# Block-sparse attention in front of a gated FFN: sampled key and value blocks gathered on GpSimd in place of dense masked scores

## The chip, the cores and the metric

The kernel runs on one core of a Trainium2 chip. The metric is device time in microseconds (us) of one execution; lower is better. The kernel before takes 371.69 us (median of three runs, 371.41 to 374.39). Engines are named as the profile names them: PE (TensorE matmuls), PEld (TensorE weight loads, which overlap PE), DVE (VectorE), ACT (ScalarE), POOL (GpSimd), SP (SyncE, which here only issues DMAs).

## The reference

The reference is a block-sparse attention over 4 batches, 8 heads, 768 tokens and head size 64, followed by a gated feed-forward network (FFN) over all 3072 tokens.

```python
block, n_blocks, window = 32, 24, 1
scores = scale * q @ k.T                                   # per batch and head, 768 x 768
mask = abs(blk_i - blk_j) <= window                        # local blocks
mask |= (blk_i == 0) | (blk_j == 0) | (blk_i == 23) | (blk_j == 23)   # global blocks
for qb in range(24):
    for kb in sampled_blocks[qb]:                          # 3 sampled key blocks a query block
        mask[qb*32:(qb+1)*32, kb*32:(kb+1)*32] = True      # same for all heads and batches
attn = softmax(where(mask, scores, -1e9))
x = (attn @ v) laid out as (3072, 512)
out = (sigmoid(x @ w_gate) * (x @ w_val)) @ w_out          # 512 -> 1536 -> 512, float32
```

Each of the 22 inner query blocks needs at most 8 of the 24 key blocks: three local, two global, three sampled. The sampled ones are known only at run time, from a tensor of 24 x 3 integers.

## The kernel before: the parts that matter

It computes all scores, takes the exponential of all of them, and multiplies by a mask of zeros and ones. Two heads share one score tile of 128 keys (twice) by 512 columns.

```python
def scores(n, p, tt):                 # n: 256 queries of a batch, p: head pair, tt: 256 keys
    st = ps.tile([128, 2, 512], f32, tag="st", bufs=2, name="st")
    for jj in range(2):
        for hd in range(2):
            nc.tensor.matmul(st[:, hd, jj*CH:(jj+1)*CH], kT[r, j, :], qT[r, 2*c:2*c+2, :], ...)
def exps(n, p, tt):                   # 144 of them
    nc.scalar.activation(pt, sts.pop((n, p, tt)), AF.Exp, scale=SCALE)
def masks(n, p, tt):                  # 144 of them
    nc.vector.tensor_tensor(pt, pt, m.unsqueeze(1).to_broadcast([128, 2, 512]), op=ALU.mult)
def values(n, p):
    # 12 matmuls of V against pt, 256 columns each (the output is already x transposed),
    # then 24 matmuls of a column of ones against pt, 128 columns each: the row sums
    # [cut]
def recips(n, p):                     # 48 of them, 128 x 128
    nc.vector.reciprocal(rz, pvz[n, p][:, CH : CH + 128])
# spread(): two matmuls copy the reciprocals to all partitions; norm(): x = xu * rb   [cut]
```

The schedule gives each slot two pieces of attention and about as much FFN work, so from the first quarter of the run on PE always has FFN matmuls to do while ACT and DVE work at the softmax:

```python
while items or s < NS:
    credit = min(credit, 0.0) + (FFN_FIRST if s < 20 else FFN_SLOT)
    # [cut: take FFN items while there is credit, interleave them with scores, exps, masks, values]
```

The softmax here doesn't subtract the row's maximum and nothing guards it: scores larger than these inputs give would overflow.

## Time and profile before

| | before |
|---|---|
| median of three runs | 371.69 us |
| span of the profiled execution | 366.4 us |
| PE, DVE, ACT, POOL busy | 318.9, 236.4, 202.3, 45.0 us |
| first FFN activation result (`h`) on DVE | 42.8 us after the start |

The page of the kernel before: each engine's busy time with its share of the span and its instructions, and three rows of the picture in 40 slices of 9.2 us (a digit is the busy tenths of a slice; PEclk is the granted TensorE clock in tenths).

```profile
PE 318.9 (87%) x3476; PEld 173.5 (47%) x3476; DVE 236.4 (65%) x395; ACT 202.3 (55%) x281; POOL 45.0 (12%) x61
...
PE   3766777758999969999999999999999998999994
...
POOL 8720022220000222200002222000000000000000
PEclk9986999999999999999999999999999999999999
```

PE is at nine tenths or more in most slices from the eleventh on and is the limit there. The chain of work that ended last, on the same page, says the same:

```profile
PE 65%; DVE 4%; ACT 3%; issue 2%; DVEq 0%
```

The costliest groups of ACT and DVE before (line, engine, operation, output and input, count; then busy us and mean ns of one; then idle time just before them and what ended it):

```profile
L228 ACT ACTIVATE pt<-st 128x1024 f16<-128x1024 f32 x144 | 146.3, 1026 | 69.8 <-PE st L217 69.6
L234 DVE TENSOR_TENSOR pt<-pt,mask 128x1024 f16<-128x1024 f16 x144 | 102.4, 711 | 63.2 <-ACT pt L228 63.2
...
L276 DVE RECIPROCAL rz<-pvz 128x128 f16<-128x128 f32 x48 | 45.9, 957 | 16.1 <-ACT xu L281 13.7
```

The exponentials and masks are large, but both groups stood idle waiting for PE: they hide behind it. A stretch of PE's timeline in the middle (start, duration, instruction) shows what PE does:

```profile
203.08 0.38 PE L355 MATMUL py<-wo,h_2356 128*128 128x512 f16 x1
203.39 0.61 PE L217 MATMUL st<-qT,kT 64*128 64x256 f16 x8
203.93 0.85 PE L247 MATMUL pvz<-pt,v_2080 128*64 128x256 f16 x12
204.70 0.52 PE L260 MATMUL pvz<-pt,ones 128*32 128x128 f16 x24
205.16 0.39 PE L323 MATMUL gv<-x_2282,wg 128*128 128x512 f16 x1
```

Matmuls are pipelined, so start-to-start times are the cost: 8 score matmuls 0.54 us, 12 value matmuls 0.77 us, 24 row-sum matmuls 0.46 us, and there is no gap. To make this kernel faster, PE must get less work, or start its full work sooner.

### The profile page before, as it was taken

To read this page: it belongs to the slowest core of one execution; us is meant where nothing else is said; L and a number is where in the kernel's file an instruction comes from. 1 tells how busy PE (TensorE), PEld (TensorE's weight loads), DVE (VectorE), ACT (ScalarE), POOL (GpSimd) and SP (SyncE) were. 2 spreads that over 40 slices of the span, in tenths; PEclk is the share of its full clock that TensorE was granted. 3 is DMA by queue.
4 is the path that set the end of the run, shared out by engine and by line. 5 is a ranking of instruction groups with operands and counts; after the bars stand their busy time and mean duration, and the time that the engine had idled before them with its cause. 6 is when DMAs were issued, how large, how long until landed. Compare 5 with 4: busy or idle time off the path is not lost.

```text
span 366.4 us, 8250 instructions
## 1 busy us (share of the span) xinstructions
PE 318.9 (87%) x3476; PEld 173.5 (47%) x3476; DVE 236.4 (65%) x395; ACT 202.3 (55%) x281; POOL 45.0 (12%) x61
## 2 busy tenths in 40 slices
PE   3766777758999969999999999999999998999994
PEld 2433545533454535445445544545554454446641
DVE  4576677777586667768657786866867677434321
ACT  1845665676666775665656666566667555221110
POOL 8720022220000222200002222000000000000000
PEclk9986999999999999999999999999999999999999
DMA  8999667760003778500004697300010000001011
GB/s 116 200 207 207 115 142 163 159 115 2 0 2 113 155 150 171 79 31 30 2 30 109 171 181 166 73 1 30 2 59 2 30 2 30 29 31 57 33 64 77
DMA packets 40897, 30.56 MB, mean 83 GB/s; under 512 B 20740, under 2 KB 37788, under 8 KB 40860
## 3 DMA queue, kind: packets, MB, share of 16 engines
q1 hardware_dynamic: 29580, 20.59, 20.5%
q0 software_dynamic: 11280, 9.44, 18.0%
q8 instruction: 27, 0.44, 0.5%
q14 instruction: 10, 0.08, 0.1%
HBM read 28.45 MB, written 6.29 MB: 95 GB/s over the span
## 4 chain that ended last, share of the span: by engine, by line
PE 65%; DVE 4%; ACT 3%; issue 2%; DVEq 0%
PE gv L323 31%; PE py L355 16%; PE pvz L247 7%; PE st L217 6%; PE pvz L260 4%; ACT pt L228 2%; DVE y L364 2%; ACT tg L334 1%; PE pvz L288 1%; DVE rz L276 1%; DVE pt L234 1%; DVE x_2282 L307 0%; ACT xu L281 0%; DVE x_2284 L307 0%; DVE h_3493 L339 0%
## 5 line engine op out<-in xcount | busy, mean ns | idle before, releaser
L228 ACT ACTIVATE pt<-st 128x1024 f16<-128x1024 f32 x144 | 146.3, 1026 | 69.8 <-PE st L217 69.6
L234 DVE TENSOR_TENSOR pt<-pt,mask 128x1024 f16<-128x1024 f16 x144 | 102.4, 711 | 63.2 <-ACT pt L228 63.2
L334 ACT ACTIVATE tg<-gv 128x512 f32<-128x512 f32 (+1 forms) x84 | 45.3, 539 | 37.9 <-PE gv L323 35.8
L276 DVE RECIPROCAL rz<-pvz 128x128 f16<-128x128 f32 x48 | 45.9, 957 | 16.1 <-ACT xu L281 13.7
L217 PE MATMUL st<-qT,kT 64*128 64x256 f16 x576 | 48.4, 278 | 6.0 <-ACT pt L228 3.7
L323 PEld LDWEIGHTS <-wv 128*128 128x128 f16 x336 | 32.8, 98 | 36.1 <-issue 6.9
L323 PEld LDWEIGHTS <-wg 128*128 128x128 f16 x336 | 28.2, 97 | 31.3 <-issue 8.0
L281 ACT COPY xu<-pvz 128x256 f32<-128x256 f32 x48 | 17.9, 373 | 33.3 <-PE pvz L260 32.5
L217 PEld LDWEIGHTS <-kT 64*128 64x128 f16 x576 | 21.9, 95 | 24.4 <-issue 15.4
L260 PE MATMUL pvz<-pt,ones 128*32 128x128 f16 x1152 | 25.5, 224 | 0.0
L364 DVE TENSOR_SCALAR y<-py 128x512 f32<-128x512 f32 x24 | 16.6, 690 | 12.1 <-PE py L355 11.1
L288 PE MATMUL pvz<-rz,sel 128*128 128x128 f16 x96 | 13.2, 218 | 12.1 <-DVE rz L276 12.1
L260 PEld LDWEIGHTS <-ones 128*32 128x32 f16 x1152 | 17.0, 98 | 9.9 <-issue 9.9
L288 PEld LDWEIGHTS <-sel 128*128 128x128 f16 x96 | 9.4, 97 | 22.7 <-issue 14.7
L137 ACT COPY qT<-ptr 128x768 f16<-128x768 f16 x4 | 3.2, 797 | 8.8 <-PE ptr L130 8.8
L196 PE MATMUL pm<-mb_127,e_70 24*128 24x256 f16 x18 | 4.3, 364 | 3.9 <-DVE mask L203 2.8
L203 DVE CAST mask<-pm 128x512 f16<-128x512 f32 x9 | 5.9, 685 | 0.8 <-PE pm L196 0.7
L105 POOL CAST q_3157<-qs 128x768 f16<-128x768 f32 x1 | 0.8, 823 | 44.9 <-DMA qs<-in_q_dram 44.9
L105 POOL CAST q_1956<-qs 128x768 f16<-128x768 f32 x1 | 0.8, 823 | 41.6 <-DVE pt L234 41.6
L323 PE MATMUL gv<-x_326,wg 128*128 128x256 f16 x12 | 3.3, 278 | 2.3 <-ACT tg L334 2.3
L323 PE MATMUL gv<-x_1478,wv 128*128 128x512 f16 x12 | 4.5, 379 | 0.7 <-ACT tg L334 0.7
L323 PE MATMUL gv<-x_3071,wv 128*128 128x512 f16 x12 | 4.5, 379 | 0.7 <-ACT tg L334 0.7
(435 smaller groups left out, 567.1 us busy)
## 6 DMA issues: line engine op xcount, KB each, us to landing
out_dram<-y SPq DMA_DIRECT2D x24, 256.0 KB, 2.0
qs<-in_q_dram SPq DMA_DIRECT2D x12, 384.0 KB, 4.6
ks<-in_k_dram SPq DMA_DIRECT2D x12, 384.0 KB, 5.0
wg<-in_moe_w_gate_dram POOLq DMA_DIRECT2D x3, 512.0 KB, 12.2
wv<-in_moe_w_val_dram POOLq DMA_DIRECT2D x3, 512.0 KB, 13.8
wo<-in_moe_w_out_dram POOLq DMA_DIRECT2D x3, 512.0 KB, 19.9
kf<-in_k_dram POOLq DMA_DIRECT2D x4, 192.0 KB, 6.7
qf<-in_q_dram POOLq DMA_DIRECT2D x4, 192.0 KB, 6.9
```

The source lines that it names most:

```text
L217: nc.tensor.matmul(st[:, hd, jj * CH : (jj + 1) * CH], kT[r, j, :], qT[r, 2 * c : 2 * c + 2, :], start=True, stop=True,)
L228: nc.scalar.activation(pt, sts.pop((n, p, tt)), AF.Exp, scale=SCALE)
L234: nc.vector.tensor_tensor(pt, pt, m.unsqueeze(1).to_broadcast([128, 2, 512]), op=ALU.mult)
L247: nc.tensor.matmul(t[hd * 64 : hd * 64 + 64, 0:CH], v_[:, hd, j, :], pts[j // 2][:, hd, (j % 2) * CH : (j % 2 + 1) * CH], start=(j == 0), ...
L260: nc.tensor.matmul(t[r0 : r0 + 32, CH : CH + 128], ones, pts[j // 2][:, hd, o : o + 128], start=False, stop=(j == NJ - 1), skip_group_chec ...
L276: nc.vector.reciprocal(rz, pvz[n, p][:, CH : CH + 128])
L281: nc.scalar.copy(xu, pvz[n, p][:, 0:CH])
L288: nc.tensor.matmul(rb[:, half * 128 : half * 128 + 128], sel[:, half, :], rz, start=True, stop=True, skip_group_check=True,)
L323: nc.tensor.matmul(t[:, 0 : cols(g)], w[:, i, f * 128 : (f + 1) * 128], xT[g, i][:, 0 : cols(g)], start=(i == 0), stop=(i == NP - 1),)
L334: nc.scalar.activation(t[:, 0 : cols(g)], pgs.pop((g, f)), AF.Tanh, scale=0.5)
L355: nc.tensor.matmul(pys[g, tt], hts[g, f][:, tt * 128 : (tt + 1) * 128], wo[:, f], start=(f == 0), stop=(f == NF - 1),)
L364: nc.vector.tensor_scalar_mul(y, pys.pop((g, tt)), 0.5)
```

## The change

The intent is to compute only the scores that the reference keeps. Per head pair (a "unit"; 16 of them, 4 a batch) the scores fall from 9 tiles of 128x1024 to 5. Local and global keys are two tiles of 128 keys for every four query blocks; the sampled blocks, three a query block, are gathered. A column of ones beside V makes the row sums a 65th column of the value matmuls. So the ones-matmuls, the big reciprocals, the spreading matmuls and most of the mask work go.

The price is on GpSimd. Each unit gathers 90 key blocks of 16 words along the free dimension (66 sampled, and 24 fixed ones, which the two-tile layout needs a second time), and for each of its two heads 30 value blocks of 32 words (22 columns of sampled blocks, 6 of fixed ones, 2 of padding). The value blocks must first be copied to all four groups of 32 partitions, by 32 SBUF-to-SBUF DMAs a batch.

```diff
+    def spread_v(b, half):                       # twice a batch, 16 DMAs each
+        for a in range(4):
+            for s in range(4):
+                nc.sync.dma_start(v4[half][32 * s : 32 * s + 32, a:NB:4]..., va[b % 2][32 * a : 32 * a + 32, ...]...)
+    def gather_k(u):                              # 2 x 45 blocks of 16 words
+        for i in range(2):
+            nc.gpsimd.indirect_copy(t...[:, 45 * i : 45 * i + 45], data, idx[:, i, 0:3], i_know_this_is_slow=True)
+    def gather_v(u):                              # 2 x 30 blocks of 32 words
+        for hd in range(2):
+            nc.gpsimd.indirect_copy(vg[u % 2][hd]...[:, :, 0 : D // 2], data[...], idx[:, 2, 0:2], i_know_this_is_slow=True)
+    def scores(u, x):                             # five pieces a unit
+        if x < 3:                                 # local keys, then the tile of fixed keys, from kg
+            ...
+                mm(i, 0, kT[u][:, t * 128 : t * 128 + 128], qs, n)
+                c = (3 * NQ + 4 * t) * BLK
+                mm(i, n, kg[u][:, c : c + 128], qs, n)
+        else:                                     # sampled keys, 64 columns a matmul
+            for r in range(16) if x == 3 else range(16, NQ):
+                mm(r // 8 % 2, r % 8 * 64, kg[u][:, c : c + 128], z[:, r + 1], 64)
+        nc.scalar.activation(pt[:, 0:w], st..., AF.Exp, scale=SCALE)
+        # [cut: masks for x < 3]
+    def values(u, half):                          # 65 columns a matmul: V and a one
+        # [cut]
+        nc.vector.reciprocal(rz, pvv[:, :, :, 64])
+    def pieces(b):                                # one batch's attention, in order
+        def prep(u):
+            return [lambda: (turn(u, "k"), gather_k(u)), lambda: (turn(u, "q"), gather_v(u))]
+        r += prep(first)
+        for u in us:
+            w = u - 1                                        # the unit before
+            a = [lambda u=u, x=x: scores(u, x) for x in (0, 1, 3, 2, 4)]
+            z = [] if u == first else ends(w)                # values, x_turn, values, x_turn of w
+            n = prep(u + 1) if u < last else []
+            for s in (a[0], z[0], a[1], n[0], z[1], a[2], z[2], a[3], n[1], a[4], z[3]):
+                if s: r.append(s)
-    # [cut: the slot-by-slot schedule with credit]
+    for s in pieces(0): s()                       # all of batch 0's attention before any FFN
+    for b in range(B):                            # batch b's FFN with batch b+1's attention mixed in
+        lo, hi = (0.5, 0.97) if b == 0 else (0.05, 0.95)
+        # [cut: pieces(b+1) spread between the fractions lo and hi of the FFN; spread_v(b+1) just before them]
+        # [cut: at the end of the block, the loads of batch b+2, issued by GpSimd]
```

`turn` transposes q or k of a unit on PE; `x_turn` transposes the attention output into the FFN's layout. FFN tiles become 384 columns wide instead of 512.

## The prediction

> **What bounds the kernel now.** The page gives PE 318.9 us busy of a 366.4 us span (87%), DVE 236.4, ACT 202.3, POOL 45.0, and the chain that ended last is 65% PE. In the slices PE is at 9 tenths or more from about 80 us on; the timeline there shows 128x512 matmuls 0.216 us apart with almost no gap. Before that PE is starved: 4.0, 6.9, 6.5, 6.8 us busy in the first four stretches of 10 us, the clock at 0.7 to 0.8 from 20 to 40 us.
>
> **What changes.** Scores fall from 144 exps of 128x1024 (1.026 us) to 80, masks from 144 (0.711 us) to 32 full and 32 part ones, the 48 reciprocals of 0.957 us become 32 tiny ones, the xu copies vanish. Added: turns of q and k on PE with copies on DVE and ACT, 32 turns of x. My sums: ACT about 145 us, DVE about 165 us. Neither was the limit, so that is worth little.
>
> PE: the FFN is the same arithmetic (384-column tiles instead of 512), about 187 us at the pitch seen. Attention now costs, per 12 score matmuls 0.66, values 0.7, sums 0.45, spread 0.21 us: about 2.0 us x 48 = 97 us. After: 640 score matmuls, half of them 64 or 128 columns wide, 1280 of 65 columns, 512 small transposes; at 25 to 55 ns each about 5.2 us x 16 = 83 us. PE work falls by only 10 to 20 us.
>
> **What is new on the critical path: GpSimd.** Each of 16 head pairs needs four gathers: 90 key blocks of 16 words, 60 value blocks of 32 words, 3360 words per partition. The trace's POOL cast (128x768, 0.82 us) gives 1.07 ns a word: 3.6 us. The Trainium skill (GPSIMD Engine Reference, Performance pitfalls for Q7 kernels) puts a small read command, one per gather index, at about 102 cycles that do not pipeline: 150 of them would be 12.8 us at 1.2 GHz; no run here shows it yet. If a command takes several indices it is a third of that. Estimate: 10 us a pair (8 to 16), 160 us in all.
>
> The whole attention of batch 0 now precedes any FFN. The first value gather waits for 6 fine-grained v loads and 16 SBUF-to-SBUF copies, about 33 us; seven more gather steps of 5 us and the last values bring the FFN's start to about 76 us, PE mostly idle and cold. Batch 1's attention is packed into the second half of the first FFN: about 10 us of stall. Later batches have about 67 us of PE work each against about 60 us of POOL work and loads: 3 to 8 us of stall each. Sum: 76 + (38 + 21 + 10) + 2 x (67 + 5) + 54 + 3, about 346, less a little for rounding up: I say 344. Each us more per pair costs about 12 us in total.
>
> **What the profile would show.** POOL busy 150 to 200 us; indirect copies of 2 to 3 us each; DVE and ACT under 50%; PE under 3 tenths until about 75 us, then above 9 tenths with dips where PE waits for kg or vg; the FFN's first matmul near 76 us.
>
> **What would make it wrong.** A gather of 4 us or more (16 us a pair): POOL then bounds every batch and the kernel is slower, near 410. Gathers of 1.5 us: near 310. Small matmuls with exposed weight loads at 80 ns rather than 40 would add 40 us.
>
> Chances: faster 0.67, within 2% 0.10, slower 0.23. Predicted 344 us, range 306 to 398.

## The result, and the profile after

The prediction was wrong in its direction: the kernel became slower.

| | before | after |
|---|---|---|
| median (four runs each) | 371.55 us | 417.37 us |
| lowest to highest | 369.38 to 374.39 | 417.13 to 418.48 |
| ratio, after over before | | 1.123 (95%: 1.116 to 1.131) |
| span of the profiled execution | 366.4 us | 416.7 us |

Some executions of a program run slower, at a lower granted clock; only fast ones are compared. A ratio here and below is the mean time of one kernel's fast runs over the mean of the other's of the same rounds, so it is not quite the ratio of the medians quoted beside it. Every experiment was timed beside the kernel before on its own chip; before's median was between 370.2 and 372.5 us in every group of runs.

The page of the kernel after (slices of 10.4 us), the same rows:

```profile
PE 313.5 (75%) x3584; PEld 193.5 (46%) x3584; DVE 176.8 (42%) x349; ACT 137.3 (33%) x193; POOL 146.4 (35%) x133
...
PE   1140656899744876969189999959699999999984
...
POOL 8415533680043544850443359024433410000000
PEclk9999756589968999998869999979699999999999
```

The chain that ended last, after:

```profile
PE 53%; issue 12%; POOL 11%; DMA 9%; DVE 8%; ACT 3%; SPq 2%; DVEq 0%; POOLq 0%
```

PE did not fill up at 80 us and stay full. It has holes in every batch, down to one tenth in the slice around 205 us. POOL is recorded as busy for only 35% of the span, yet POOL, "issue" and DMA now hold 32% of the chain where before "issue" alone had 2%. The groups that answer to those shown of before, and the new ones of GpSimd:

```profile
L331 ACT ACTIVATE pt<-st 128x1024 f16<-128x1024 f32 (+1 forms) x80 | 79.8, 1002 | 148.3 <-PE st L296 148.2
...
L342 DVE TENSOR_TENSOR pt<-pt,mask 128x1024 f16<-128x1024 f16 (+1 forms) x64 | 39.4, 636 | 115.5 <-ACT pt L331 115.4
L277 POOL INDIRECT_COPY vg<-v,idx 128x960 uint32 x32 | 57.8, 1807 | 76.6 <-issue 48.1
...
L262 POOL INDIRECT_COPY kg<-kT,idx 128x720 uint32 x32 | 39.4, 1232 | 109.8 <-issue 51.4
```

The intended savings are all there: 67 us less of exponentials, 63 us less of masks, and the 45.9 us of reciprocals became 6.2. They were off the critical path and bought nothing directly. And the two gather groups have about 50 us each of idle time before them, called "issue", in which the engine waited for nothing that the profile shows. What PE waited for (what, for which releaser, us in total, times, longest):

```profile
PE st L296 <- POOL kg L262: 57.1, 12, 12.9
PE st L296 <- DVE qz L256: 9.6, 5, 5.4
```

Twelve waits for gathered keys make up 57.1 us; no other wait comes near.

### Where the 73 us between prediction and result lie

DVE's `h` instruction ends each FFN step, 24 of them a batch. So the start of the 1st, 25th, 49th and 73rd `h` cut the run into a head, three blocks (one batch's FFN with the next batch's attention mixed in) and a rest. These cuts are used for every experiment below. The predicted row is the prediction's sum: an FFN start at 76 us and about 3 us to the first `h`, and its terms for the blocks.

| us | head, to first `h` | block of batch 0 | block 1 | block 2 | rest |
|---|---|---|---|---|---|
| predicted | 79 | 69 | 72 | 72 | 54 |
| after | 88.4 | 90.0 | 90.5 | 85.5 | 62.2 |
| missed by | +9.4 | +21.0 | +18.5 | +13.5 | +8.2 |

(The predicted row adds up to 346, which I had rounded to 344; the after row adds up to the span of 416.7, within rounding.) Each of the three blocks, not just the head, is far longer than predicted. The rest is 8 us longer for reasons that no experiment moves: it is 62 to 63 us in all of them. In the trace the matmuls there are as fast as I had summed: the eight of an FFN step take 1.30 us, and four output matmuls 0.86 us. What my 54 + 3 left out are stalls: about 0.23 us at every fourth step, and 0.95 us before each of the last three outputs, where PE waits until DVE has read the one `py` buffer; together 4.2 us. The run also ends 5 us after the last matmul, not 3. Most of what is left of the 8 us is the cut: the first `h` comes only 1.5 us after the FFN's start there, not 3.

### How long is a gather?

GpSimd's timeline in the head of the kernel after (start, duration, instruction, idle time before it and what ended that):

```profile
14.66 1.20 POOL L262 INDIRECT_COPY kg<-kT,idx 128x720 uint32 x1 [2.31 <-issue]
17.95 1.20 POOL L262 INDIRECT_COPY kg<-kT,idx 128x720 uint32 x1 [2.08 <-issue]
27.95 1.60 POOL L277 INDIRECT_COPY vg<-v,idx 128x960 uint32 x1 [8.80 <-DMA v<-va]
31.31 1.60 POOL L277 INDIRECT_COPY vg<-v,idx 128x960 uint32 x1 [1.77 <-issue]
```

The same view later, where batch 2's attention is computed:

```profile
186.98 1.20 POOL L262 INDIRECT_COPY kg<-kT,idx 128x720 uint32 x1 [2.09 <-issue]
197.59 1.88 POOL L277 INDIRECT_COPY vg<-v,idx 128x960 uint32 x1 [9.41 <-PE gv L434]
201.24 1.60 POOL L277 INDIRECT_COPY vg<-v,idx 128x960 uint32 x1 [1.77 <-issue]
204.91 1.20 POOL L262 INDIRECT_COPY kg<-kT,idx 128x720 uint32 x1 [2.07 <-issue]
```

A key gather is recorded as 1.20 us, but two of them in a row start 3.29 us apart (14.66 and 17.95); two value gathers start 3.36 us apart. The Trainium skill (Perfetto Trace Analysis, GPSIMD Engine Instruction) says that a GpSimd span is unreliable and that consecutive instructions should be timed by the spacing of their starts; this trace agrees, and by a factor of more than two. A unit's four gathers so take 2 x 3.28 + 2 x 3.37 = 13.3 us, where I had predicted 10.

### What does PE wait for?

The second of these timelines is the heart of the case. PE, in the same place:

```profile
199.28 0.27 PE L296 MATMUL st<-qz,kT 128*128 128x256 f16 x1
209.45 0.40 PE L296 MATMUL st<-qz,kg 128*128 128x256 f16 x1 [9.90 <-POOL kg L262]
```

PE stood still for 9.9 us for the key gathers of batch 2's second unit. The keys to be gathered lay ready: DVE copied that kT at 193.54, for 0.95 us. But the key gathers had been issued behind the value gathers of the first unit, and those waited for the spread copies of V. SP issued these 32 copies one by one:

```profile
182.13 22.96 SPq L144 DMA_DIRECT2D v<-va  x32
```

The 16th, the last that the first unit needs, was issued at 193.17 us and landed at 195.46; the value gather's record begins 2.1 us later, of which 1.77 us is the gap that precedes any such gather here. (The timeline names "PE gv L434" as what ended that wait. It is an inference from semaphores, and the copies explain the time better.) The Trainium skill (TensorE: Matmul & The Clock Gate, Part 1) says that GpSimd's queue is strictly first in, first out, on each of its cores; the trace agrees, as the key gathers, ready at about 194.5 us, did not begin until the two value gathers were done, at about 202.8.

So there were two theories after the result. **Size**: the gathers are a third longer than predicted, and POOL is simply the limit. **Order**: GpSimd has time enough, but things are issued in an order in which one waiting gather holds up another and PE behind it. A third, **data**: the loads and the spread of V come late, and the gathers only show it.

### The profile page after: what moved, and what is told of

The parts are those of the page before. It is cut to its first block, busy times and chain, and to the rows that moved or that the text cites. A ratio compares the mean times of both kernels' runs of the same rounds, so it can differ in the third digit from the quotient of the medians.

```text
span 416.7 us, 8409 instructions
## 1 busy us (share of the span) xinstructions
PE 313.5 (75%) x3584; PEld 193.5 (46%) x3584; DVE 176.8 (42%) x349; ACT 137.3 (33%) x193; POOL 146.4 (35%) x133
## 3 DMA queue, kind: packets, MB, share of 16 engines
q1 hardware_dynamic: 30640, 19.53, 19.4%
## 4 chain that ended last, share of the span: by engine, by line
PE 53%; issue 12%; POOL 11%; DMA 9%; DVE 8%; ACT 3%; SPq 2%; DVEq 0%; POOLq 0%
PE gv L434 23%; PE py L454 14%; PE st L296 7%; DMA v<-va 7%; POOL kg L262 6%; PE pv L357 6%; POOL vg L277 3%; SPq L144 2%; ACT pt L331 2%; PE ptr L245 2%; DVE pt L342 2%; DVE kT L251 1%; DMA va<-in_v_dram 1%; POOL va L135 1%; DVE y L463 1%
## 5 line engine op out<-in xcount | busy, mean ns | idle before, releaser
L331 ACT ACTIVATE pt<-st 128x1024 f16<-128x1024 f32 (+1 forms) x80 | 79.8, 1002 | 148.3 <-PE st L296 148.2
L296 PE MATMUL st<-qz,kg 128*128 128x64 f16 (+1 forms) x448 | 45.5, 228 | 62.9 <-POOL kg L262 57.1
L342 DVE TENSOR_TENSOR pt<-pt,mask 128x1024 f16<-128x1024 f16 (+1 forms) x64 | 39.4, 636 | 115.5 <-ACT pt L331 115.4
L277 POOL INDIRECT_COPY vg<-v,idx 128x960 uint32 x32 | 57.8, 1807 | 76.6 <-issue 48.1
L445 DVE SCALAR_TENSOR_TENSOR h<-tg,gv 128x384 f16<-128x384 f32 x96 | 53.1, 553 | 74.0 <-PE gv L434 66.3
L434 PE MATMUL gv<-x,wg 128*128 128x384 f16 x384 | 82.4, 339 | 0.0
L434 PE MATMUL gv<-x,wv 128*128 128x384 f16 x384 | 80.7, 334 | 1.8 <-DVE h L445 1.0
L443 ACT ACTIVATE tg<-gv 128x384 f32<-128x384 f32 x96 | 47.0, 490 | 100.1 <-PE gv L434 86.7
L262 POOL INDIRECT_COPY kg<-kT,idx 128x720 uint32 x32 | 39.4, 1232 | 109.8 <-issue 51.4
L454 PE MATMUL py<-wo,h 128*128 128x512 f16 x288 | 75.5, 389 | 2.9 <-DVE y L463 2.9
L434 PEld LDWEIGHTS <-wv 128*128 128x128 f16 x384 | 38.4, 100 | 32.7 <-issue 10.4
L434 PEld LDWEIGHTS <-wg 128*128 128x128 f16 x384 | 36.8, 101 | 25.3 <-issue 3.8
L463 DVE TENSOR_SCALAR y<-py 128x512 f32<-128x512 f32 x24 | 16.5, 688 | 11.0 <-PE py L454 10.9
```

Source lines behind the costliest of these rows:

```text
L262: nc.gpsimd.indirect_copy(t.rearrange("p n r -> p (n r)") .bitcast(u32) .rearrange("p (n r) -> p n r", r=BLK // 2)[:, 45 * i : 45 * i + 45 ...
L277: nc.gpsimd.indirect_copy(vg[u % 2][hd] .rearrange("p n e -> p (n e)") .bitcast(u32) .rearrange("p (n e) -> p n e", e=VE // 2)[:, :, 0 : D ...
L296: nc.tensor.matmul(st[:, bank, col : col + n], keys, qs, start=True, stop=True)
L331: nc.scalar.activation(pt[:, 0:w], st.rearrange("p a n -> p (a n)")[:, 0:w], AF.Exp, scale=SCALE)
L342: nc.vector.tensor_tensor(pp, pp, mk.unsqueeze(2).to_broadcast([128, 2 * nt, 2, nq]), op=ALU.mult)
L434: nc.tensor.matmul(t, w[:, i, f * 128 : (f + 1) * 128], xT[g, i], start=(i == 0), stop=(i == NP - 1),)
```

## The experiments

Eighteen more kernels ran. All differ from the kernel after, or from an earlier experiment, by the edits shown. "Wrong" means that the result is wrong because work was taken away; all others were correct. The letters in the quoted expectations are the names of theories that were current then, as explained in each.

### Taking the gathers away: e1, e6, e8

```diff
 def gather_k(u):
-    t = work.tile(...)
-    for i in range(2): nc.gpsimd.indirect_copy(...)
+    t = kgs[u % 2]            # memset once, on GpSimd (e1); one tile for all, on DVE (e6)
 def gather_v(u):
-    for hd in range(2): nc.gpsimd.indirect_copy(...)
+    return
 # e8: as e6, and spread_v returns at once
```

> All 64 gathers on GpSimd are taken out (kg and vg are set once; wrong result on purpose); loads, spreads, scores, exps, values and FFN stay. Theory G (the gathers' own time, 3.3 to 3.9 us from one to the next in the trace of after, is what was mis-sized, and everything waits in that line): the FFN starts near 45 us instead of 86 and the time falls from 417 to about 310 us. Rival D (the data's way is the cost: fine-grained v loads, 32 SBUF-to-SBUF copies a batch, the late loads): it stays above 370 us. Rival P (the many small matmuls and the cold clock): above 380.

> e1_no_gathers again with its flaw mended: there the added memsets on GpSimd held DVE, and so PE, for about 13 us in the head. Now DVE clears them while it waits for its first load. Expected 342 to 348 us, the FFN's first h at about 62 us instead of 75. That would still be 30 us above the 310 that the prediction's sums give for free gathers; those 30 us would then be the order (attention of a whole batch before any FFN, pieces packed into half a block), not GpSimd.

> e6_no_gathers_b without the 128 copies v<-va as well (nothing reads them there). If the data's way (DMA traffic and SP's issue of 20 to 29 us a batch) holds what is left above 310 us, 20 us or more below e6. If not, within 5 us of e6.

All three are wrong. e1 measured 357.49 us (ratio to before 0.959). It had a flaw of its own: the memsets that I put on GpSimd held up DVE and PE in the head (PE waited 18.3 us for `qz`), some 13 us of it on the path. e6, with the memsets on DVE, measured 344.89 us (0.932), as expected. e8 measured 344.58 us (0.929). None of the three times in e1's expectation came: about 310 (gathers), above 370 (data) or above 380 (small matmuls and cold clock).

So the gathers cost 417.4 - 344.9 = 72.5 us in the kernel after. Without gathers the spread of V makes no difference, as nothing then waits for it. And without gathers the stages are:

| us | head | block 0 | block 1 | block 2 | rest |
|---|---|---|---|---|---|
| predicted | 79 | 69 | 72 | 72 | 54 |
| e6, no gathers | 62.9 | 74.6 | 71.4 | 71.4 | 62.6 |
| after | 88.4 | 90.0 | 90.5 | 85.5 | 62.2 |

This is uncomfortable for the prediction in a useful way: 344 us, the predicted time, is the time of the kernel with free gathers. In the full blocks I had allowed 3 to 8 us for the gathers' stalls above 67 us of PE work; they cost 14 to 19 us above a floor of 71.4.

Not all of this is waiting. In block 1 of the kernel after, PE idled for 16.5 us and was busy for 74.0; in e6 it idled for 1.7 and was busy for 69.6, with the same matmuls. So about 4 of the 19 us are slower matmuls: the granted clock was 0.92 in that block, and 1.00 in e6. Over the whole run PE was busy for 313.5 us against 297.1. In these runs a wait cost more than its own length.

### Taking only the spread of V away: e3

```diff
 def spread_v(b, half):
+    return
-    nc.vector.memset(v4[i][:, NB], 0.0)
+    nc.gpsimd.memset(v4[i], 0.0)
```

> The 128 SBUF-to-SBUF copies v<-va are taken out (v4 is zeroed once; wrong result on purpose); the gathers stay. Theory G: only the first value gathers of a batch come sooner, 8.8 us in the head and up to 14 us in batches 2 and 3 together; in all 10 to 22 us less, about 400. Rival D: 40 us or more less, under 377.

Wrong; 409.83 us (1.101). This too was flawed: the memset on GpSimd delayed the first key load by about 9 us (PE waited 15.4 us for it instead of 6.3), so without the flaw it would stand at about 401, an estimate. By that estimate the spread alone accounts for 16 of the 72 us. The theory "data" is not enough.

### What does one gather cost? e4 and e5

```diff
 # e4: the same 90 key blocks, split otherwise
-for i in range(2):                                        # 45 + 45
+for c0, c1, n0, n1 in ((0, 4, 0, 60), (4, 6, 60, 90)):    # 60 + 30
 # e5: smaller gathers
-    [:, 45 * i : 45 * i + 45]     (keys)      [:, :, 0 : D // 2]  (values, 32 words a block)
+    [:, 45 * i : 45 * i + 36]                 [:, :, 0 : D // 4]  (16 words a block)
```

> The same 90 key blocks gathered as 60 + 30 instead of 45 + 45; the result is right. From the two shapes in the trace of after (45 x 16 words: 2.08 us of gap and 1.20 us of record; 30 x 32 words: 1.77 and 1.60) I fit: a gather costs 1.15 us + 0.0207 us per index + 0.00167 us per word, the index part lying in the unrecorded gap. Then the 60 takes 2.39 + 1.60 us and the 30 takes 1.77 + 0.80 us, and the time stays within 1% of after. If the gap is a fixed dispatch cost instead, both have the same gap near 2 us.

> The gathers are cut to the size that the prediction took: with 0.27 us + 31 ns per index + 2.25 ns per word, fitted to the three shapes seen in after and e4_split_60_30, two key gathers of 36 x 16 words and two value gathers of 30 x 16 words are 10.0 us a pair instead of 13.3 (wrong result on purpose). If the size of a gather was the whole miss (theory G), the time is the predicted 344, within 10 us. If the gathers are only part of it, as e1_no_gathers says (about 5.5 us of total per us a pair), it is about 398.

e4 is correct: 419.40 us (one run, state unknown). e5 is wrong: 391.01 us (1.053). GpSimd's timeline of e4:

```profile
37.11 1.40 POOL L263 INDIRECT_COPY kg<-kT,idxk 128x960 uint32 x1 [2.91 <-issue]
39.79 1.00 POOL L263 INDIRECT_COPY kg<-kT,idxk 128x480 uint32 x1 [1.28 <-issue]
```

And of e5:

```profile
51.78 1.08 POOL L268 INDIRECT_COPY kgs<-kT,idx 128x576 uint32 x1 [1.60 <-issue]
```

(Its value gathers, 30 blocks of 16 words, show a gap of 1.28 us and a record of 1.01.) The unrecorded gap grows and shrinks with the gather, and the gap before a gather belongs to that gather. With the gap counted in:

| blocks x words a block | gap + record, us | 0.27 + n x (0.0313 + 0.00225 x words) |
|---|---|---|
| 45 x 16 (keys, after) | 2.08 + 1.20 = 3.28 | 3.30 |
| 60 x 16 (e4) | 2.91 + 1.40 = 4.31 | 4.31 |
| 30 x 16 (e4, e5) | 1.28 + 1.00 = 2.28 | 2.29 |
| 30 x 32 (values, after) | 1.77 + 1.60 = 3.37 | 3.37 |
| 36 x 16 (e5) | 1.60 + 1.08 = 2.68 | 2.69 |
| 24 x 32 (e10, below) | 1.31 + 1.43 = 2.74 | 2.75 |

The constants were worked out from the first four rows; the last two test them. (The first fit, in e4's expectation, was wrong: it gave 2.39 + 1.60 us for 60 blocks.) A unit's 13.3 us are thus 3360 words at 2.25 ns (7.6 us), 150 indices at 31 ns (4.7 us) and 4 starts at 0.27 us (1.1 us). I had taken 1.07 ns a word from a cast and put the remaining 6.4 us on commands: the words cost twice what I thought, the indices less. The figure that I quoted from the Trainium skill, about 102 cycles for a small read command that does not pipeline (85 ns at its 1.2 GHz, an estimate), is not what an index costs here: 31 ns, or 67 ns with its 16 words. The measurement decides.

With e5's gathers a unit takes 2 x 2.68 + 2 x 2.28 = 9.9 us, almost exactly the predicted 10. The kernel then takes 391.0 us, neither the 344 nor the 398 of its expectation. So of the miss, 417.4 - 391.0 = 26 us is the size of the gathers (about 8 us for each us of a unit, in this range), and 47 us is something else. "Size" is part of it and not the larger part.

### The order of issue: e2 and e9

e2 only starts batch 1's attention earlier in batch 0's FFN. e9 adds the theory of order: issue the key gathers of a batch's first two units ahead of the first value gather, which is the one that waits for the spread of V.

```diff
 # e2
-        lo, hi = (0.5, 0.97) if b == 0 else (0.05, 0.95)
+        lo, hi = (0.25, 0.97) if b == 0 else (0.05, 0.95)
 # e9: e2, and
-        r += prep(first)
+        r += [
+            lambda: (turn(first, "k"), gather_k(first)),
+            lambda: turn(first, "q"),
+            lambda: (turn(first + 1, "k"), gather_k(first + 1)),
+            lambda: gather_v(first),
+        ]
         for u in us:
             n = prep(u + 1) if u < last else []
+            if u == first: n[0] = None          # its key gather is already issued
```

> Only the place changes where batch 1's attention begins within batch 0's FFN: after 25% of it instead of 50%. In the trace of after, GpSimd sits idle from 92.6 to 115.0 us because the turn of k stands there in PE's order, and then needs 55 us in a row. If that idle time is on the critical path (theory S, order), batch 1's first gather starts near 97 us and the time falls by 12 to 20 us, to 398 to 405. If batch 1 waits for its data anyway (rival D), under 5 us.

> Correct result, same work. e2_early, and in each batch the key gather of the second head pair goes ahead of the value gather of the first, which waits for the copies v<-va. GpSimd takes its work in order, so in after and e2_early that key gather stood behind a value gather that waited 9 us in the head and 8 to 9 us in each later batch. If that head-of-line wait is on the critical path (theory S), 15 to 30 us less than e2_early: 382 to 396. If the rate of GpSimd or PE's own order binds (rival R), within 5 us of e2_early, at about 407.

e2: 410.60 us (1.104), correct; a gain of 7 where I expected 12 to 20, for the first value gather of batch 1 then waited 8.5 us for the spread of V. e9: 389.19 us (1.049), correct and within the expected range: 21 us from the order alone. GpSimd's timeline in e9, at the place that corresponds to the 9.9 us wait:

```profile
176.67 1.20 POOL L262 INDIRECT_COPY kg<-kT,idx 128x720 uint32 x1 [2.60 <-issue]
180.22 1.29 POOL L262 INDIRECT_COPY kg<-kT,idx 128x720 uint32 x1 [2.34 <-issue]
183.96 2.08 POOL L277 INDIRECT_COPY vg<-v,idx 128x960 uint32 x1 [2.45 <-DMA v<-va]
```

And PE's timeline there:

```profile
186.09 0.19 PE L357 MATMUL pv<-vg,pt 128*128 128x65 f16 x1 [2.19 <-POOL vg L277]
```

The key gathers now run while V is being spread, and the scores follow. PE's wait here is 2.2 us, with one of 3.1 us for the second head's values after it, where it was 9.9. PE's two largest waits in e9, in all:

```profile
PE st L296 <- POOL kg L262: 23.7, 8, 6.6
PE pv L357 <- POOL vg L277: 19.4, 7, 3.6
```

Its waits for gathered keys fell from 57.1 to 23.7 us. But a new wait appears, 19.4 us for gathered values: PE too takes its matmuls in order here, and the values of a unit stand in front of the next unit's scores. That became the next theory.

### Loading earlier: e7

The loads of batch b+2 are issued only at the end of a block. e7 moves loads and spread copies of the next batch into the block before it, one unit at a time, on top of e2.

```diff
+  # after the value gather of a batch's first unit: load_v(b+1), load_qk(b+1, 0 and 1)
+  # after that of the second: spread_v(b+1, 0), load_qk(b+1, 2); of the third: load_qk(b+1, 3)
+  # at the last scores of the batch: spread_v(b+1, 1)
-  # loads of b+2 at the end of a block; spread_v(b+1) just before pieces(b+1), for b > 0
```

> Correct result, same work. Batch 1's attention begins at 25% as in e2_early; loads of batch b+2 and the copies v<-va are issued while batch b+1 is being worked on instead of after it, so that the first gathers of batches 2 and 3 need not wait (they waited 9 and 15 us for data in after, and the gathers idled 20 to 30 us between batches). Theory S (these waits between batches are on the critical path): the two later blocks fall from 88 and 83 us to about 72 each, the time to 380 to 388. If GpSimd's own rate binds there (four pairs of 13.3 us and 10 us of DMA issue against 67 us of PE work), or PE waits move elsewhere, over 398.

412.31 us (1.113), correct: no gain over e2's 410.60, and on the side that the expectation gives to GpSimd's own rate or to waits that move elsewhere (over 398). PE's waits for gathered keys were 62.6 us, where e2 has 56.6. GpSimd issues these loads itself, about 11 us a batch, and now does it amid the gathers that PE waits for: in block 0, ten loads stand between two gathers from 132.84 to 140.69 us, and that block grew from 86.5 us in e2 to 94.7, while block 2 fell from 84.7 to 80.6. This fits early data that help a later block, and an issue of loads that costs more than that; no run separates the two.

### Gathering less: e10

The 24 fixed key blocks and 6 fixed value columns of each unit are known when the kernel is written, so they need no gather. e10 is e9 with three DVE copies a unit for the keys and three a batch for the values. The first three score pieces then need no gathered keys at all, so they go first. (`pt` also has 9 buffers instead of 10.)

```diff
+    def beta_k(u):            # kT -> kb: 3 nc.vector.tensor_copy, for the fixed key tile
+    def beta_v(b):            # va -> vb: 3 nc.vector.tensor_copy a batch
-   gathers: 45 + 45 key blocks, 2 x 30 value blocks a unit
+   gathers: 33 + 36 key blocks, 2 x 24 value blocks a unit
-   mm(i, n, kg[u][:, c : c + 128], qs, n)
+   mm(i, n, kbs[u][:, t * 128 : t * 128 + 128], qs, n)
-   a = [... for x in (0, 1, 3, 2, 4)]
+   a = [... for x in (0, 1, 2, 3, 4)]
```

> Correct result. e9_order, and the 24 key blocks and 6 value slots that are the same for every input leave the gathers: DVE copies them into tiles of their own, so a pair's gathers shrink to 33 + 36 key indices and 2 x 24 value indices, 10.7 us instead of 13.3 by the fitted costs, and the first three of the five score pieces of a pair no longer wait for GpSimd. Both theories of the loss (gather size, order) say faster than e9: 360 to 380. If it is no faster than e9, the waits for GpSimd were not the limit.

372.85 us (1.008, interval 1.000 to 1.016), correct and in the range: 16 us less than e9, and level with the kernel before. A unit's gathers take 2.49 + 2.68 + 2 x 2.74 = 10.7 us by the law above. What PE waits for in e10:

```profile
PE pv L379 <- POOL vg L300: 22.5, 9, 3.8
...
PE st L319 <- POOL kg L285: 3.7, 2, 2.7
```

The waits for keys are nearly gone; those for values remain. By the cuts, 10 of the 16 us are in the head. Shorter gathers and the pieces that need none came in one edit, so how the 16 us divide between them was not settled.

One more thing shows in e10, a gather that runs while DVE copies `vb` (the second of these):

```profile
87.68 1.04 POOL L285 INDIRECT_COPY kg<-kT,idx 128x528 uint32 x1 [8.70 <-DVE qz L255]
90.44 3.84 POOL L285 INDIRECT_COPY kg<-kT,idx 128x576 uint32 x1 [1.73 <-issue]
```

It is recorded as 3.84 us; an undisturbed one of the same size is 1.08. DVE was busy with the three `vb` copies from 90.31 to 93.65. The Trainium skill (GPSIMD Engine Reference, Key points) says that GpSimd shares its SBUF interfaces with VectorE. The trace fits: all four gathers beside `vb` copies were slow, and in e13 below, which takes these copies off DVE, the longest of that size is 1.57 us. In the other direction, a 128x1024 mask multiplication on DVE took 692 ns on average in e6 without gathers, 727 with those of e10, and 893 in the kernel after, where the longest took 2.77 us and the median is still 693.

### Loading earlier again: e11

e11 is e10 with e7's earlier loads: with the key waits gone, perhaps late data matter now.

> e10_static with the loads and copies of the next batch issued during this one, as in e7_prefetch. There it gained nothing because GpSimd had 71 us of work per batch including 10 us of DMA issue; here it has about 55. If that was the reason, the two later blocks come down to the 71 us of e6_no_gathers_b, and the time to 352 to 368. If it is slower than or equal to e10, the mid-batch DMA issues delay the gathers more than early data helps.

373.74 us (1.010), correct: no gain, against the 5 to 21 us expected. I was wrong about early loads twice.

### Placing the values behind the next scores: e12, e17, e18

If PE waits at `values` of the last unit while the next unit's scores could run, the values should stand later in PE's order. One line moves them (it also brings `n[0]`, the turn and gather of the next unit's keys, ahead of the values; the two were not separated):

```diff
-            for s in (a[0], z[0], a[1], n[0], z[1], a[2], z[2], a[3], n[1], a[4], z[3]):
+            for s in (a[0], a[1], n[0], a[2], z[0], a[3], z[1], z[2], n[1], a[4], z[3]):
 # e12 = e10 with this line; e17 = the kernel after with it alone; e18 = e9 with it
```

> Correct result. e10_static with the values of the pair before placed after the third score piece instead of the first, so that PE has 10 us more before it needs vg. If PE's order is what is left (theory S), most of the 22.5 us of PE waits for vg goes and the time falls by 5 to 12 us, to 361 to 368. If the copies on DVE are, within 3 us of e10's 373.

> Correct result. The change itself with one line changed: values after the third score piece. In after PE waits 57 us for the key gather and hardly for vg, because the first score piece of a pair needs the keys; if so, moving the values gives under 8 us: 409 to 418. If it gives 15 us or more, the place of the values was a cause of its own.

> Correct result. e9_order with the values later, gathers unchanged at 13.3 us a pair. If order is all that was wrong, it comes near e12: under 365. If the shorter gathers and the score pieces freed of them are needed too, 378 to 390.

e12: 355.60 us (0.957, 353.86 to 356.88), correct, better than expected, and faster than both kernels. e17: 413.30 us (1.118), correct and as expected. e18: 377.22 us (1.016, interval 1.006 to 1.025), correct, and just below the 378 to 390 of "shorter gathers are needed too".

| values' place | kernel after (e17) | with the order of e9 (e18) | with order and fewer gathered blocks (e12) |
|---|---|---|---|
| before | 417.37 | 389.19 | 372.85 |
| after moving | 413.30 | 377.22 | 355.60 |
| gain | 4 | 12 | 17 |

The same line is worth 17 us in one place and at most a little in another: the 4 us of e17 are not clear of noise (ratios of 1.106 to 1.130 and 1.116 to 1.131). In e17 PE still waits for keys, and placing values later cannot help with that:

```profile
PE st L296 <- POOL kg L262: 59.0, 12, 13.0
```

In e12 both waits are small, and PE has no deep hole left after the head. The PE row of its page, in slices of 8.8 us:

```profile
PE   1445864799779999999899999898999999999983
```

And what PE waits for in e12:

```profile
PE st L319 <- POOL kg L285: 10.4, 6, 3.5
PE pv L379 <- POOL vg L300: 9.2, 6, 2.9
```

The stages, from the kernel after to e12, beside the floor without gathers:

| us | head | block 0 | block 1 | block 2 | rest |
|---|---|---|---|---|---|
| after | 88.4 | 90.0 | 90.5 | 85.5 | 62.2 |
| e9 | 83.5 | 80.9 | 80.9 | 80.7 | 62.2 |
| e10 | 73.5 | 77.3 | 79.2 | 79.2 | 62.3 |
| e12 | 73.8 | 72.6 | 72.2 | 72.8 | 62.3 |
| e6, no gathers | 62.9 | 74.6 | 71.4 | 71.4 | 62.6 |

In e12 the blocks are at the floor; the 10.7 us that remain above e6 are in the head, where gathers run with no FFN to hide them.

The gain is not all shorter waiting. From e10 to e12 PE's idle time (span less busy time) fell by 12.6 us and its busy time by 5.2. From e9 to e18 the idle time stayed (75.8 and 75.1 us) and the busy time fell from 312.4 to 301.8, 6 us of it in the head, at a granted clock of 0.70 and then 0.79. So e18's gain shows as faster matmuls; what raised the clock there is not settled.

### Taking DVE's copies out of the gathers' way: e13, e14, e15, e16

e13 is e10 with the `vb` copies made by DMAs on SP, so that they don't run beside gathers. e14 is e12 and e13 together. e15 is e14 with early loads, e16 is e12 with early loads.

```diff
 def beta_v(b):
-    nc.vector.tensor_copy(t[0:64, 0:5], src[0:64, 1:6])            # and two more
+    nc.sync.dma_start(flat(t[0:64, 0:5]), flat(src[0:64, 1:6]))    # and two more, ahead of spread_v(b)
```

> Correct result. e10_static with the 12 copies of the known value blocks (0.9 to 1.2 us each on DVE) made by 12 DMAs on SP ahead of the copies v<-va. Theory S: within 4 us of e10 (2 us of SP issue go before the spread). If DVE's copies and their meeting with a gather are what is left: 8 us or more less, below 365, and no gather of 3.85 us.

> Correct result. Both edits. 357 to 365 us if they add; that would be 2 to 4% faster than before's 371. No lower than e12 if the copies cost nothing.

> Correct result. e14_both with the loads and copies v<-va of the next batch issued during this one, as in e11. With the waits for vg gone there may be something left to gain: 352 to 362 us if data still comes late, equal to e14 or slower if the DMA issues amid the gathers cost as much as early data gains, as in e11.

> Correct result. e12_values_later with early loads. The two full blocks have 1 to 2 us left above free gathers, so early data can give at most 4 us: 352 to 358. Slower if the DMA issues amid the gathers cost more, as in e15.

All four are correct. e13: 374.75 us (1.009), 2 us from e10 and not faster, with no gather above 1.92 us: the slowed gather is not on the path, or costs no more than what replaced it (PE's waits for gathered values rose from 22.5 to 34.7 us). e14: 363.00 us (0.978), in the expected range but 7 us slower than e12. Its DMAs go ahead of the spread of V on SP, and PE's waits for gathered values rose from 9.2 to 22.2 us. e15: 363.92 us (0.979), no better than e14. e16: 363.73 us (0.980), 8 us slower than e12, with waits for gathered keys at 16.4 instead of 10.4 us. Early loads were tried four times, each time with another schedule around them, and gained nothing each time. The cuts show where: block 0, which carries the issue of these loads but has no early data itself, grew every time (e7 by 8.2 us, e11 by 3.0, e15 by 8.5, e16 by 8.2), and blocks 1 and 2 together changed by -5.0, -2.3, -6.4 and +1.6 us.

## Why the prediction was wrong, point by point

**What bounds the kernel before: right.** PE is the limit, and ACT and DVE were not. ACT fell to 137.3 us (predicted 145), DVE to 176.8 (165), and this bought nothing.

**PE's new work: about right.** PE's busy time fell by 5 us in the kernel after, where its clock is often low, and by 16 us in e12; I had said 10 to 20. The small matmuls were not a problem: sixteen score matmuls of 64 columns took 0.63 us at full clock, under 40 ns each, within the 25 to 55 ns predicted. In the head they took 1.01 us three times: at 48 and 76 us at a granted clock of 0.5, and at 22 us, where the record of the clock still says 1.0. The Trainium skill (TensorE: Matmul & The Clock Gate, Part 1) says that an idle array runs at half clock and reaches full clock only after about 3.4 us of work; this case shows a half clock with a factor of 1.6 at the first two places, and a mean of 0.66 between 40 and 85 us of the kernel after, but no run checks the 3.4 us.

**The size of the gathers: a term mis-sized.** I predicted 10 us a unit; they take 13.3. The step was "The trace's POOL cast (128x768, 0.82 us) gives 1.07 ns a word: 3.6 us". A gathered word takes 2.25 ns, and a cast is no measure for it. This cost 26 us (after against e5). The sensitivity in the prediction, about 12 us for each us per pair, was measured as 8. "Indirect copies of 2 to 3 us each" was too short by the spacing of starts, 3.3 us. POOL's recorded 146.4 us is just under the predicted 150 to 200, but as more than half of each gather is not recorded, that figure can't be read as work.

**The blocks: the step that failed.** The prediction says: "Later batches have about 67 us of PE work each against about 60 us of POOL work and loads: 3 to 8 us of stall each." This compares two sums of busy time, as if two engines with enough time each would overlap. What the runs showed in its place is a chain of three queues, each strictly in order. SP issues 32 spread copies in 23 us; the first value gather waits for 16 of them; the next unit's key gathers stand behind that gather on GpSimd; the scores, which need those keys, stand in front of ready FFN work on PE. With gathers as short as I had predicted (e5), blocks 1 and 2 still took 84.1 and 81.4 us instead of 72. Reordering alone, with the gathers unchanged (e2 to e9), took 21 us off, and moving the values then took another 12 (e18): 40 us in all from order alone, against 26 from shorter gathers alone. But order alone left blocks 1 and 2 at 76.7 and 78.0 us (e18). With 10.7 us a unit, three of five score pieces freed of gathered keys, and the new order (e12) they took 72.2 and 72.8 us, which is what I had predicted. So the sums could be reached, but not by the schedule of the change, and the order of issue was there to be read before the run.

**The head.** Predicted 76 us to the FFN's first matmul, measured 85.57. With e5's gathers it came at 76.27 us, as predicted, so this miss is the gathers' size. That PE would be under three tenths until then was wrong: it is at five to eight tenths from 42 us on, on a low clock.

**Batch 0's block.** Predicted 69 us with 10 us of stall. Even without gathers it takes 74.6 us, so about 6 us of the miss has nothing to do with them. I put it down to attention packed into the second half of that FFN, which no run tests alone.

**The rest.** Predicted 54 us by the cuts above; it takes 62 to 63 us in every kernel of this family. That is a mis-sized term (stalls and the run's end, as above) that has nothing to do with the gathers.

**What would make it wrong.** "A gather of 4 us or more ... near 410": it came to 417 with gathers of 3.3 us. The warning named the right engine but the wrong mechanism, so the range, up to 398 us, was too narrow.

What stays open: what GpSimd does in the gap before a gather's record; how e10's 16 us divide between shorter gathers and pieces that need none; and whether the head's last 11 us above the floor can be hidden.

## What to carry to other kernels

When a change moves work to an engine that also waits for data, don't compare sums of busy time: write down the order of issue on each queue, find the first instruction that must wait, and ask what stands behind it on that engine and on every engine that it feeds. Time an unfamiliar GpSimd instruction by the spacing of consecutive starts, in a run of its own, before a prediction rests on it. And expect repairs of such a chain to be worth little until the wait ahead of them is gone: the same line moved here gave about 4 us alone, not clear of noise, and 17 us last.

## What the Trainium skill lacked or had wrong

- GPSIMD Engine Reference, Performance pitfalls for Q7 kernels: about 102 cycles for each small read command, "e.g. one per gather index". For the indirect copies here an index cost 31 ns and a word 2.25 ns, so 67 ns for a block of 16 words, less than the estimated 85 ns of 102 cycles at 1.2 GHz. Whether an indirect copy issues one such command an index, no run shows.
- No page that I found gives the cost of an indirect copy. The runs show 0.27 us + blocks x (31 ns + 2.25 ns x words a block), for 24 to 60 blocks of 16 or 32 words on 128 partitions, to within 0.02 us.
- Perfetto Trace Analysis, GPSIMD Engine Instruction: it rightly says to time by start-to-start spacing. It does not say that the part left out grows with the instruction: a gap of 1.28 us before 30 blocks and 2.91 us before 60, which the profile calls "issue" and which looks like idle time.
- No page that I found gives the time that SyncE needs to issue a copy by the copy's shape: 32 SBUF-to-SBUF copies took 22.96 us here, 0.72 us each, which set when the first value gather could start.
